# Scores of four steps in one block of 64x64 tiles, in a kernel of windowed attention and a two-layer MLP

## The chip, the core and the metric

The kernel runs on one core of one Trainium2 chip. A core has a matrix engine (TensorE, "PE" in the profile, with its weight loads as "PEld"), VectorE ("DVE"), ScalarE ("ACT"), GpSimd ("POOL") and SyncE ("SP"), each with its own queue of instructions, done in order. Matmuls read SBUF and write PSUM, which has eight banks of 128 partitions x 512 fp32 values. TensorE's 128x128 array can be split into tiles that work at the same time: a matmul on half of the columns writes 64 partitions, one on half of the rows reads 64 partitions. The metric is the device time of one execution in microseconds.

## What is computed

Attention with a symmetric window of 32 positions (8 batches, 8 heads, 576 tokens, 64 values a head), and on its output an MLP with a squared relu:

```python
scores = scale * np.matmul(q, k.transpose(0, 1, 3, 2))      # q, k, v: (8, 8, 576, 64)
mask = np.abs(pos[:, None] - pos[None, :]) <= 32
scores = np.where(mask, scores, -1000000000.0)
...
attn = np.exp(scores)
attn = attn / (np.sum(attn, axis=-1, keepdims=True) + 1e-09)
return np.matmul(attn, v).astype(np.float32)
...
x = np.ascontiguousarray(attn_out.transpose(0, 2, 1, 3)).reshape(B * S, H * D)   # (4608, 512)
r = np.maximum(x @ w_in, 0.0)                               # w_in: (512, 2048)
return (r * r @ w_out).astype(np.float32)                   # w_out: (2048, 512)
```

## The kernel before

**Attention steps.** The work of attention is cut into 72 steps, nine per batch: step n = 9 b + c takes 64 queries of all eight heads against 128 keys (64 queries plus 32 to each side; for even c the key halves are swapped). `scores` issues eight matmuls (L491), for four pairs of heads j and two key halves u, each with 64 weight columns of K on half of the array's columns and 128 moving columns of Q. K's 128 rows hold two heads, so Q (`QZ`) is kept twice for each pair, with zeros in the rows of the other head: columns 0 to 63 give the first head and 64 to 127 the second. The 128x512 result lies in one of two banks (`SC`). ScalarE takes its exp (L496) into `E`, VectorE multiplies by the mask (L503) into `PT`; both have two buffers. `av` does P V in eight matmuls of 65 columns, the last of which is the row sum (L518), into the bank `AVP`; VectorE takes the reciprocals (L530) and normalises (L532) into `XR`. `xturn` turns that so that the MLP can read it (`XT`, 32 slots of 64 tokens): on TensorE through the bank `TRP` and ScalarE for steps below 27 (L552, L557), and from 27 on, for two steps at once, by a transposing DMA on SP's queue (L543).

**Inputs.** For the first two batches K, Q and V come in pieces of 128 tokens (64 for the last), W1 in four chunks of 512 columns and W2 in four of 512 rows, all by DMAs that GpSimd issues in the order of the list `FIRST` ("k", "q", "v" with batch and piece, "e" the edge of V, "a" a W1 chunk, "b" a W2 chunk). K and Q of these batches are turned on TensorE through the score banks (`fine_turn`, L374). From the third batch on, GpSimd loads them raw, VectorE turns them in blocks of 32x32 (L451), and 16 DMAs a batch on SP's queue (`spread`, L465) bring them to their rows, in `KT` and `QZ`, which have two buffers each.

**MLP.** The 4608 tokens are nine tiles of 512. `mm1` is the first layer: a unit fills one of two banks `HT` (they alternate with the unit's number k), ScalarE does the relu (L581) into one of four buffers `RT`, and the square goes to VectorE, or to ScalarE for every second unit in the range `SQ` (L586). Tile 0 is done in 16 smaller units, in the order of `UNITS`: (first token, tokens, first block of the hidden width). Those of 128 tokens use the undivided array, all other matmuls of the kernel two column tiles. `mm2` is the second layer, four segments for each 128 tokens into one of two banks `OUTP`; ScalarE copies the result out and issues its DMA.

**Order.** Nothing of the order is written out by hand. Each instruction group is recorded with the tiles that it reads and writes, a guessed duration and a key; a planner (`Prog.schedule`) then plays the engines and DMA queues forward in time, takes on each engine the ready group with the smallest key, and adds 95 ns where TensorE's tiling changes. The resulting order is what each engine gets, with semaphore waits for what the tiles demand. While TensorE would have nothing to do at the start, it gets matmuls on the zero tile `ZZ`. The keys come from the constants at the head of the file: `LEAD` (how many steps attention runs ahead of the MLP), `LB` (a shift per batch), `QB`, `WB`, `VB`, `TB`, `GB`, `TST` and `SK` (when raw Q and K, V, its copies, the turns and the spreads of a batch are due), `FK`, `FQ`, `VK0`, `VK1` (pieces of the first batches), `KM`, `MD`, `TM` (MLP).

Of the kernel before, what the change touches and what calls it, by code (L numbers as in the profile page):

```python
# [5 lines left out]
ALU = mybir.AluOpType  # L6
ACTF = mybir.ActivationFunctionType
# [13 lines left out]
LEAD = 11  # L21
# [6 lines left out]
LB = (5.75, 0.0, -0.25, -3.0, -0.75, 3.75, 2.25, 1.0)  # L28
TB = (22.5, -1.0, -5.0, -4.5, 15.5, 29.5)
GB = (86.0, 56.0, 67.0, 42.0, 58.0, 11.0)  # L30
TST, SK = 0.7, -27.0
QB = (70.0, 34.0, 26.0, -78.0, 102.0, 86.0)
WB = (3.0, 26.0, 54.0, 80.0, 89.0, 54.0)
VB = (30.5, -13.5, 14.0, -32.5, 0.5, 0.5)
SQ = (16, 144, 2)
VENG = ('DVE', 'DVE', 'DVE')
KENG = ('DVE', 'ACT')
FK, FQ = 29.75, 18.0
VK0, VK1 = 9.25, 8.0
KM, MD, TM = -55.0, 8.0, 3.0  # L40
# [5 lines left out]
FIRST = (  # L46
# [222 lines left out]
class Gen:  # L269
# [5 lines left out]
    def alloc(self):  # L275
        nc = self.nc
        sb, ps = nc.alloc_sbuf_tensor, nc.alloc_psum_tensor
        self.SC = [ps(f"sc{i}", [128, 512], F32) for i in range(2)]
        self.AVP = ps("avp", [128, 512], F32)
        self.TRP = ps("trp", [128, 1024], BF16)  # L280
# [14 lines left out]
        self.E = [sb(f"e{i}", [128, 512], BF16) for i in range(2)]  # L295
        self.PT = [sb(f"pt{i}", [128, 512], BF16) for i in range(2)]
# [67 lines left out]
    def fine_turn(self, b, t, x, key):  # L364

        t0, n = PIECES[x]
        tag, ps = ("sc", t == "q"), self.SC[t == "q"][:]
# [112 lines left out]

    def scores(self, n):
        b, c = divmod(n, NCH)
        i = b % 2
        sc = self.SC[n % 2]
        key = n - LEAD + LB[b]

        def f(e):
            for j in range(4):
                for u in range(2):
                    at = 64 * c + 64 * (u if c % 2 else 1 - u)  # L490
                    mm = e.matmul(sc[64 * u:64 * u + 64, 128 * j:128 * j + 128], self.KT[i][:, j, at:at + 64],  # L491
                                  self.QZ[i][:, j, :, 64 * c:64 * c + 64], start=True, stop=True)
            return mm

        self.p.rec("PE", f, reads=self.qk_tags(b, c), writes=[("sc", n % 2)], key=key, dur=230, mode="col")
        self.p.rec("ACT", lambda e: e.activation(self.E[n % 2][:], sc[:], ACTF.Exp, scale=0.125),  # L496
                   reads=[("sc", n % 2)], writes=[("e", n % 2)], key=key, dur=600)
        mi = 0 if c % 2 else (2 if c == 0 else 3 if c == NCH - 1 else 1)
        msk = self.MASK[mi]
        pt = self.PT[n % 2][:].rearrange("p (h q) -> p h q", h=8)  # L500
        ee = self.E[n % 2][:].rearrange("p (h q) -> p h q", h=8)
        mb = bass.AP(msk, 0, [[64, 128], [0, 8], [1, 64]])
        self.p.rec("DVE", lambda e: e.tensor_tensor(pt, ee, mb, ALU.mult),  # L503
                   reads=[("e", n % 2), ("mask", mi)], writes=[("pt", n % 2)], key=key, dur=430)

    def av(self, n):
        b, c = divmod(n, NCH)
# [229 lines left out]
```

## Time and profile before

| | |
|---|---|
| median of 3 runs | 312.55 us (311.18 to 313.21) |
| the profiled execution | 312.32 us, its span in the profile 310.5 us |
| granted TensorE clock | 1.0 |
| matmuls and weight loads | 4117 of each |
| DMA traffic | HBM read 36.70 MB, written 9.44 MB |

A row of the groups reads: line, engine and operation, tile written <- tiles read, shape, count | busy us in all, mean ns of one | idle time just before them, and what ended most of it. A row of the timeline: start us, length us, engine, line, operation, tiles, shape, count. Matmuls overlap, so the length of a row exceeds the distance to the next start. A row of the stretches: from:to, its length, then for each engine that has such instructions (here PE, PEld, DVE, ACT) the busy us and count, then granted clock, DMA share and GB/s. A row of DMA issues: tiles, queue, count, KB each, median us from issue to landing.

### The profile page before, as it was taken

The numbers are of one execution on the slowest core, as the hardware profiler recorded it, in microseconds if no ns is written. First come the engines' busy times: TensorE is split into PE (matmuls) and PEld (weight loads), VectorE is DVE, ScalarE is ACT, GpSimd is POOL, SyncE is SP. The second block draws the span as 40 slices with busy tenths as digits, with TensorE's granted clock in tenths as the row PEclk, the third lists the DMA queues.
The fourth block names the chain that finished last, engine by engine and source line by source line (L and its number), as shares of the span: only waits on it lengthen the run. The fifth ranks groups of instructions, "written<-read, shape, count | busy, mean of one in ns | idle before, by whom it ended". The sixth has DMA issues, their size and how long they took to land.

```text
span 310.5 us, 9706 instructions
## 1 busy us (share of the span) xinstructions
PE 301.4 (97%) x4117; PEld 222.4 (72%) x4117; DVE 184.4 (59%) x460; ACT 200.9 (65%) x374; POOL 89.1 (29%) x129
## 2 busy tenths in 40 slices
PE   6879999999999999999999999999999999999996
PEld 2548887868977777776577777777777776776665
DVE  7667467957888988868859645688463232111000
ACT  2557698776866883588377857888746862675211
POOL 8999958331153242431222121000000000000000
PEclk9999999999999999999999999999999999999999
DMA  9999999999989989998889496314232012000112
GB/s 69 146 174 197 175 199 186 228 190 223 179 116 198 169 84 152 260 190 101 138 153 186 94 141 54 73 48 109 68 103 70 3 51 87 34 36 36 68 73 98
DMA packets 99226, 38.51 MB, mean 124 GB/s; under 512 B 71920, under 2 KB 94192, under 8 KB 99184
## 3 DMA queue, kind: packets, MB, share of 16 engines
q0 software_dynamic: 73664, 18.36, 62.7%
q1 hardware_dynamic: 20480, 10.36, 15.8%
q10 hardware_dynamic: 5040, 9.18, 9.1%
q8 instruction: 32, 0.52, 0.7%
q14 instruction: 10, 0.08, 0.1%
HBM read 36.70 MB, written 9.44 MB: 149 GB/s over the span
## 4 chain that ended last, share of the span: by engine, by line
PE 82%; DMA 7%; DVE 5%; POOL 4%; SPq 1%; issue 1%; ACT 0%; POOLq 0%; DVEq 0%
PE outp L62 37%; PE ht L62 33%; PE sc L491 5%; PE avp L518 3%; PE ht L60 3%; DMA vd<-in_v_dram 3%; DMA qz<-qst 2%; DVE kst L451 2%; DVE qst L451 2%; DMA kt<-kst 2%; POOL qfr L361 1%; SPq L465 1%; POOL kfr L361 1%; POOL vd L409 1%; PE trp L552 1%; PE sc L374 1%
## 5 line engine op out<-in xcount | busy, mean ns | idle before, releaser
L62 PE MATMUL outp<-w,gt 128*64 128x512 bf16 (+1 forms) x1184 | 140.4, 373 | 0.0
L62 PE MATMUL ht<-xt,w 128*64 128x512 bf16 (+1 forms) x1280 | 132.3, 348 | 0.5 <-issue 0.4
L581 ACT ACTIVATE rt<-ht 128x512 bf16<-128x512 f32 x144 | 85.3, 595 | 40.6 <-PE ht L62 35.4
L62 PEld LDWEIGHTS ht<-xt,w 128*64 128x64 bf16 x1280 | 93.5, 136 | 22.5 <-issue 1.3
L62 PEld LDWEIGHTS outp<-w,gt 128*64 128x64 bf16 x1184 | 74.7, 110 | 32.7
L586 DVE TENSOR_TENSOR gt<-rt 128x512 bf16<-128x512 bf16 x80 | 33.7, 422 | 47.9 <-ACT rt L581 40.4
L496 ACT ACTIVATE e<-sc 128x512 bf16<-128x512 f32 x72 | 41.6, 595 | 14.4 <-PE sc L491 8.7
L409 POOL DMA_DIRECT2D vd<-in_v_dram x32 | 29.2, 922 | 56.4 <-PE avp L518 37.1
L604 ACT ACTIVATE oe<-outp 128x512 f32<-128x512 f32 x35 | 20.9, 596 | 33.3 <-PE outp L62 33.1
L586 ACT ACTIVATE gt<-rt 128x512 bf16<-128x512 bf16 x64 | 40.4, 631 | 1.5 <-PE outp L62 0.3
L451 DVE STREAM_TRANSPOSE kst<-kraw 128x256 bf16<-128x256 bf16 (+1 forms) x48 | 36.7, 828 | 1.8 <-DMA kt<-kst 1.8
L451 DVE STREAM_TRANSPOSE qst<-qraw 128x256 bf16<-128x256 bf16 (+1 forms) x48 | 35.6, 833 | 1.8 <-DMA qz<-qst 1.8
L530 DVE RECIPROCAL rs<-avp 128x4 f32<-128x4 f32 x72 | 13.0, 181 | 35.2 <-PE avp L518 34.6
L503 DVE TENSOR_TENSOR pt<-e,mask 128x512 bf16<-128x512 bf16 x72 | 29.6, 412 | 5.8 <-ACT e L496 4.8
L532 DVE TENSOR_TENSOR xr<-avp,rs 128x256 bf16<-128x256 f32 x72 | 30.3, 420 | 1.1
L491 PE MATMUL sc<-qz,kt 128*64 128x128 bf16 x576 | 26.5, 220 | 0.9 <-DVE kt L384 0.6
L491 PEld LDWEIGHTS sc<-qz,kt 128*64 128x64 bf16 x576 | 22.4, 110 | 6.4 <-DVE kt L384 1.1
L417 POOL DMA_DIRECT2D vx<-in_v_dram x16 | 10.1, 630 | 32.4 <-PE sc L491 17.0
L429 DVE COPY vx<-vd 64x528 bf16<-64x528 bf16 (+1 forms) x28 | 16.4, 586 | 3.9 <-DMA vd<-in_v_dram 3.4
L400 POOL DMA_DIRECT2D kraw<-in_k_dram x24 | 14.9, 689 | 10.4 <-DVE kst L451 10.4
L400 POOL DMA_DIRECT2D qraw<-in_q_dram x24 | 15.1, 703 | 4.1 <-DVE gt L586 2.8
L390 ACT ACTIVATE qz<-sc,half 128x512 bf16<-128x512 bf16 (+1 forms) x20 | 12.0, 644 | 6.5 <-PE sc L374 6.3
(43 smaller groups left out, 160.8 us busy)
## 6 DMA issues: line engine op xcount, KB each, us to landing
out_dram<-oe ACTq DMA_DIRECT2D x35, 256.0 KB, 2.8
vd<-in_v_dram POOLq DMA_DIRECT2D x32, 128.0 KB, 6.2
kraw<-in_k_dram POOLq DMA_DIRECT2D x24, 144.0 KB, 12.7
qraw<-in_q_dram POOLq DMA_DIRECT2D x24, 144.0 KB, 10.9
kt<-kst SPq DMA_DIRECT2D x48, 72.0 KB, 4.0
qz<-qst SPq DMA_DIRECT2D x48, 72.0 KB, 4.0
w<-in_moe_w_in_dram POOLq DMA_DIRECT2D x4, 512.0 KB, 10.2
w<-in_moe_w_out_dram POOLq DMA_DIRECT2D x4, 512.0 KB, 16.1
```

The lines of the kernel that those rows point to most:

```text
L62: mm = e.matmul(out[r:r + 64], w[:, r:r + 64], x, start=start, stop=stop)
L400: self.p.rec("POOL", lambda e, g=g, s=s: e.dma_start(raw[32 * g:32 * g + 32], s), writes=[("raw", t, b % 2, g)], dma=(f"{t}{b % 2}", b), k ...
L409: self.p.rec("POOL", lambda e, s=s: e.dma_start(self.VD[i][:, s, :, 0:64], v[b, :, 32 + 128 * s:160 + 128 * s, :].rearrange("h p d -> p h ...
L429: self.p.rec(on, lambda e, d=dst, c=src: e.tensor_copy(d, c) if on == "DVE" else e.activation(d, c, ACTF.Copy), reads=rd, writes=[("vxc", ...
L451: self.p.rec("DVE", lambda e: e.transpose(dst, src), reads=[("raw", t, i, g) for g in range(4)], writes=[("st", t, dh, m0)], key=key, dur= ...
L491: mm = e.matmul(sc[64 * u:64 * u + 64, 128 * j:128 * j + 128], self.KT[i][:, j, at:at + 64], self.QZ[i][:, j, :, 64 * c:64 * c + 64], star ...
L496: self.p.rec("ACT", lambda e: e.activation(self.E[n % 2][:], sc[:], ACTF.Exp, scale=0.125), reads=[("sc", n % 2)], writes=[("e", n % 2)], ...
L503: self.p.rec("DVE", lambda e: e.tensor_tensor(pt, ee, mb, ALU.mult), reads=[("e", n % 2), ("mask", mi)], writes=[("pt", n % 2)], key=key, ...
L532: self.p.rec("DVE", lambda e: e.tensor_tensor(bass.AP(xr, o, [[512, 128], [64, 4], [1, 64]]), bass.AP(self.AVP, 0, [[512, 128], [VE, 4], [ ...
L581: self.p.rec("ACT", lambda e: e.activation(rt[:], ht[:], ACTF.Relu), reads=[("ht", k % 2)], writes=[("rt", k % 4)], key=key, dur=600)
L586: self.p.rec(on, lambda e: e.tensor_tensor(dst, rr, rr, ALU.mult) if on == "DVE" else e.activation(dst, rr, ACTF.Square), reads=[("rt", k ...
L604: self.p.rec("ACT", lambda e: e.activation(oe[:], op[:], ACTF.Copy), reads=[("outp", x % 2)], writes=[("oe", x % 3)], old=[("mtmp", 0), (" ...
```

## The change

The scores of steps 32 to 71 are made in groups of four steps. A group is one block of 64 matmuls on four tiles of 64x64: the array's row halves r hold the two heads of a pair, so that each head's 64 rows of K meet only its own 64 rows of Q, and the zeros in `QZ` aren't read. A matmul has 64 moving columns in place of 128. The row halves write to different banks of a pair. There are two pairs: the two score banks, and a second one from the banks of the row turns and of P V; the group's first two steps go to the first pair and the other two to the second. The exp of a step then reads 256 values from each bank of its pair, and what follows finds its columns in another order. `E` and `PT` get four buffers each. Steps below 32 are computed as before.

```diff
+    def score_group(self, n0):
+        def f(e):
+            for n in range(n0, n0 + 4):
+                b, c = divmod(n, NCH)
+                kt, qz, sc = self.KT[b % 2], self.QZ[b % 2], self.PAIR[n // 2 % 2]
+                o = 256 * (n % 2)
+                for j in range(4):
+                    for u in range(2):
+                        at = 64 * c + 64 * (u if c % 2 else 1 - u)
+                        for r in range(2):
+                            mm = e.matmul(sc[64 * u:64 * u + 64, r, o + 64 * j:o + 64 * j + 64], kt[64 * r:64 * r + 64, j, at:at + 64],
+                                          qz[64 * r:64 * r + 64, j, r, 64 * c:64 * c + 64], start=True, stop=True)
+            return mm
...
+        self.p.rec("PE", f, reads=list(dict.fromkeys(rd)), writes=[("sc", 0), ("sc", 1), "trp", "avp"],
+                   key=n0 - LEAD + LB[n0 // NCH] - GK, dur=448, mode="quad")
...
+        else:
+            if n % 4 == 0:
+                self.score_group(n)
+            sc, tags = self.PAIR[n // 2 % 2][:, :, 256 * (n % 2):256 * (n % 2) + 256], [[("sc", 0), ("sc", 1)], ["trp", "avp"]][n // 2 % 2]
...
-                self.scores(n)
-                self.av(n)
-                self.xturn(n)
+                if n < NG:
+                    ns = [n]
+                elif n % 4 == 3:
+                    ns = range(n - 3, n + 1)
...
+                for n in ns:
+                    self.scores(n)
+                for n in ns:
+                    self.av(n)
+                    self.xturn(n)
```

A relu that overwrites a buffer which ScalarE itself has squared now waits for that square by semaphore:

```diff
+        if k % 4 in self.squared:
+            relu.deps.add(self.squared.pop(k % 4))
```

And the constants of the planner are others; the order of every engine comes out anew. Those that the text speaks of:

```diff
-LEAD = 11
+LEAD = 12
...
-TST, SK = 0.7, -27.0
+TST, SK = 0.8, 5.0
...
-SQ = (16, 144, 2)
+SQ = (12, 112, 2)
...
+NG, GK = 32, -5.0
...
 UNITS = (
-    (0, 128, 0), (128, 128, 4), (128, 128, 12), (128, 128, 8), (256, 256, 2), (0, 128, 4), (256, 256, 6),
-    (256, 256, 10), (256, 256, 12), (256, 256, 14), (0, 128, 8), (256, 256, 0), (128, 128, 0), (0, 128, 12),
-    (256, 256, 4), (256, 256, 8),
+    (128, 128, 12), (0, 128, 0), (256, 256, 0), (128, 128, 4), (256, 256, 12), (256, 256, 4), (256, 256, 10),
+    (0, 128, 12), (128, 128, 8), (256, 256, 14), (0, 128, 4), (128, 128, 0), (256, 256, 2), (0, 128, 8),
+    (256, 256, 6), (256, 256, 8),
 )
 FIRST = (
-    ("v", 0, 1), ("k", 0, 0), ("q", 0, 0), ("k", 0, 2), ("q", 0, 1), ("k", 0, 1), ("v", 0, 2), ("q", 0, 2),
-    ("q", 0, 3), ("v", 0, 0), ("q", 1, 1), ("e", 0, False), ("a", 0, 2), ("k", 1, 2), ("v", 0, 3),
-    ("k", 0, 3), ("a", 0, 1), ("q", 0, 4), ("v", 1, 3), ("k", 0, 4), ("a", 0, 0), ("a", 0, 3), ("k", 1, 0),
-    ("b", 0, 0), ("q", 1, 0), ("k", 1, 1), ("e", 0, True), ("q", 1, 2), ("k", 1, 4), ("v", 1, 0),
-    ("e", 1, False), ("k", 1, 3), ("b", 0, 1), ("b", 0, 2), ("v", 1, 2), ("v", 1, 1), ("e", 1, True),
-    ("b", 0, 3), ("q", 1, 3), ("q", 1, 4),
+    ("q", 0, 0), ("k", 0, 0), ("q", 0, 1), ("k", 0, 2), ("q", 0, 2), ("k", 0, 1), ("k", 0, 3), ("v", 0, 0),
+    ("q", 0, 3), ("v", 0, 1), ("k", 1, 1), ("v", 0, 2), ("e", 0, False), ("a", 0, 3), ("v", 0, 3),
+    ("q", 0, 4), ("k", 0, 4), ("a", 0, 0), ("q", 1, 0), ("q", 1, 1), ("a", 0, 1), ("v", 1, 3), ("k", 1, 0),
+    ("e", 0, True), ("v", 1, 0), ("k", 1, 2), ("a", 0, 2), ("b", 0, 2), ("e", 1, False), ("b", 0, 1),
+    ("e", 1, True), ("q", 1, 3), ("v", 1, 2), ("v", 1, 1), ("b", 0, 0), ("q", 1, 2), ("k", 1, 3), ("q", 1, 4),
+    ("k", 1, 4), ("b", 0, 3),
 )
```

More of the change, by code (lines that the diff above doesn't have):

```diff
@@ L294, in alloc @@
         self.ID = sb("ident", [128, 128], BF16)
[L295 to L296 removed]
+        self.E = [sb(f"e{i}", [128, 512], BF16) for i in range(4)]
+        self.PT = [sb(f"pt{i}", [128, 512], BF16) for i in range(4)]
         self.RS = [sb(f"rs{i}", [128, 4], F32) for i in range(2)]
@@ L483, in scores @@
         i = b % 2
-        sc = self.SC[n % 2]
         key = n - LEAD + LB[b]
[L487 to L495, printed above, removed]
@@ L496, in scores, with f @@
-        self.p.rec("ACT", lambda e: e.activation(self.E[n % 2][:], sc[:], ACTF.Exp, scale=0.125),
-                   reads=[("sc", n % 2)], writes=[("e", n % 2)], key=key, dur=600)
+        ex = self.E[n % 4][:]
+        if n < NG:
+            sc, tags = self.SC[n % 2], [("sc", n % 2)]
+            def f(e):
+                for j in range(4):
+                    for u in range(2):
+                        at = 64 * c + 64 * (u if c % 2 else 1 - u)
+                        mm = e.matmul(sc[64 * u:64 * u + 64, 128 * j:128 * j + 128], self.KT[i][:, j, at:at + 64],
+                                      self.QZ[i][:, j, :, 64 * c:64 * c + 64], start=True, stop=True)
+                return mm
+            self.p.rec("PE", f, reads=self.qk_tags(b, c), writes=tags, key=key, dur=230, mode="col")
+        else:
+            if n % 4 == 0:
+                self.score_group(n)
+            sc, tags = self.PAIR[n // 2 % 2][:, :, 256 * (n % 2):256 * (n % 2) + 256], [[("sc", 0), ("sc", 1)], ["trp", "avp"]][n // 2 % 2]
+            ex = ex.rearrange("p (r x) -> p r x", r=2)
@@ L498, in scores @@
+        self.p.rec("ACT", lambda e: e.activation(ex, sc, ACTF.Exp, scale=0.125),
+                   reads=tags, writes=[("e", n % 4)], key=key, dur=600)
         mi = 0 if c % 2 else (2 if c == 0 else 3 if c == NCH - 1 else 1)
         msk = self.MASK[mi]
-        pt = self.PT[n % 2][:].rearrange("p (h q) -> p h q", h=8)
-        ee = self.E[n % 2][:].rearrange("p (h q) -> p h q", h=8)
+        pt = self.PT[n % 4][:].rearrange("p (h q) -> p h q", h=8)
+        ee = self.E[n % 4][:].rearrange("p (h q) -> p h q", h=8)
@@ L580, in mm1 @@
         us = range(t0 // 128, (t0 + n) // 128)
-        self.p.rec("ACT", lambda e: e.activation(rt[:], ht[:], ACTF.Relu), reads=[("ht", k % 2)],
-                   writes=[("rt", k % 4)], key=key, dur=600)
+        relu = self.p.rec("ACT", lambda e: e.activation(rt[:], ht[:], ACTF.Relu), reads=[("ht", k % 2)],
+                          writes=[("rt", k % 4)], key=key, dur=600)
+        if k % 4 in self.squared:
+            relu.deps.add(self.squared.pop(k % 4))
         rr = rt[:].rearrange("p (d t) -> p d t", d=nd)
```

55 lines of the change are left out of this document (31 added, 24 removed).

## The prediction

> **What bounds the kernel now.** I read the page's busy table and chain of waits first, to see which engine sets the end, and then the groups by shape, to see how much of that engine's time the scores hold.
>
> ```profile
> span 310.5 us, 9706 instructions
> PE 301.4 (97%) x4117; PEld 222.4 (72%) x4117; DVE 184.4 (59%) x460; ACT 200.9 (65%) x374; POOL 89.1 (29%) x129
> ...
> PE 82%; DMA 7%; DVE 5%; POOL 4%; SPq 1%; issue 1%; ACT 0%; POOLq 0%; DVEq 0%
> ...
> L62 PE MATMUL outp<-w,gt 128*64 128x512 bf16 x1120 | 136.9, 379 | 0.0
> L62 PE MATMUL ht<-xt,w 128*64 128x512 bf16 x896 | 108.4, 380 | 0.5 <-issue 0.4
> L491 PE MATMUL sc<-qz,kt 128*64 128x128 bf16 x576 | 26.5, 220 | 0.9 <-DVE kt L384 0.6
> ```
>
> TensorE is the bound: 97% busy, 82% of the chain. Its rows hold almost no idle time (0.5 and 0.9 us). "Busy" counts overlapping matmuls, though, so what a block really costs is read from start to start in the timeline, in a stretch without a wait:
>
> ```profile
> 177.79 0.42 PE L491 MATMUL sc<-qz,kt 128*64 128x128 bf16 x8
> 178.01 0.32 PE L518 MATMUL avp<-vx,pt 128*64 128x65 bf16 x8
> 178.14 1.06 PE L62 MATMUL outp<-w,gt 128*64 128x512 bf16 x8
> 179.00 0.42 PE L491 MATMUL sc<-qz,kt 128*64 128x128 bf16 x8
> ```
>
> One step's scores cost 0.22 us, one step's P V 0.13, eight matmuls of 512 columns 0.86. So 2016 of the long matmuls take 2016 x 0.86/8 = 217 us and 72 score blocks 72 x 0.22 = 16 us. Time that TensorE is spared in the packed part comes off the span one for one. The next view says where the packed part begins: the idle-filling matmuls on the zero tile, by stretch.
>
> ```profile
> 0.00:20.00 20.00, 12.49 (x75) 4.64 (x77) 0.27 (x1) 0.91 (x4) 1.00 1.62 120
> 20.00:40.00 20.00, 4.44 (x32) 1.45 (x28) 0.00 (x0) 0.00 (x0) 1.00 1.69 188
> 40.00:310.00 270.00, 0.00 (x0) 0.00 (x0) 0.00 (x0) 0.00 (x0) 1.00 0.77 120
> ```
>
> Fillers stand only before 40 us, 4.44 us of them between 20 and 40. There the kernel has spare TensorE time; after it, next to none.
>
> **The tiles, part one: the block itself.** Steps 32 to 71 are 40 steps, ten groups. A group drops 4 x 8 matmuls of 128 columns, 4 x 0.22 = 0.89 us, and adds 64 of 64 columns on four tiles, 16 rounds of four. No 64-row tile is in this trace. The nearest row is a block with 64 moving and 64 weight columns on two tiles:
>
> ```profile
> 53.62 0.29 PE L374 MATMUL sc<-ident,kfr 128*64 128x64 bf16 x8
> 53.74 0.39 PE L62 MATMUL outp<-w,gt 128*64 128x512 bf16 x2
> ```
>
> Eight in 0.12 us, 0.0305 us a round of two, weights hidden. If four tiles run as two do, a group is 16 x 0.0305 = 0.49 us. Bounds: at half of a score block it is 4 x 0.11 = 0.45; if the two row halves don't overlap, it is 32 rounds, 0.98; and if the sequencer's rate in the P V block above (16 weight loads and matmuls in 0.13 us, 8 ns each) is its best, 128 instructions take 1.02. I take 0.49, as that row has the same shape. The page "TensorE: Matmul & The Clock Gate" of the Trainium skill, Part 3, puts packed tiles about 4 ns apart; by an estimate from it, 128 instructions would take 0.51 us and the change would keep its gain. The trace's 8 ns stretch has only two tiles to fill, so it is no proof of a limit, but no row here shows 4 ns either.
>
> **Part two: the mode switches.** The group stands between two-tile blocks, so it costs two changes of tiling. Where the first MLP tile changes between 128x128 and two tiles, the trace shows such changes:
>
> ```profile
> 40.84 0.41 PE L491 MATMUL sc<-qz,kt 128*64 128x128 bf16 x8
> 41.19 1.08 PE L60 MATMUL ht<-xt,w 128*128 128x128 bf16 x16
> 42.20 0.41 PE L491 MATMUL sc<-qz,kt 128*64 128x128 bf16 x8
> 42.45 0.39 PE L62 MATMUL ht<-xt,w 128*64 128x256 bf16 x4
> ```
>
> The score block ahead of the change takes 0.35 us in place of 0.22: 0.12 to 0.13 for a change. Two per group are 0.24. The bounds are nothing (if that gap is special to 128x128) and 0.3. The page "TensorEngine Tiling (Array Packing)" of the Trainium skill, Key Properties, says that a changed tiling mode drains the engine; it speaks against the change, and would charge these 20 changes as the row does.
>
> So a group costs 0.49 + 0.24 = 0.73 against 0.89: 0.16 to 0.17 saved, **1.7 us over ten groups**, with +3.7 us (1.02 + 0.24 = 1.26) as the bad end and -2.4 (0.45 + 0.2) as the good one.
>
> **What hangs on the group.** The exp of a step reads two banks in place of one, still 128x512; P V reads the same number of columns in another order: nothing. The group writes both the score pair and the pair that holds P V's output, so P V of its first step now waits for the exps of its third and fourth. Queued behind that on ScalarE are relus, and behind P V's wait on TensorE the MLP matmuls, which the written order puts ahead where it can.
>
> ```profile
> L496 ACT ACTIVATE e<-sc 128x512 bf16<-128x512 f32 x72 | 41.6, 595 | 14.4 <-PE sc L491 8.7 <-DVE pt L503 5.6
> L586 ACT ACTIVATE gt<-rt 128x512 bf16<-128x512 bf16 x64 | 40.4, 631 | 1.5 <-PE outp L62 0.3
> L586 DVE TENSOR_TENSOR gt<-rt 128x512 bf16<-128x512 bf16 x80 | 33.7, 422 | 47.9 <-ACT rt L581 40.4 <-PE outp L62 7.1
> ```
>
> Four exps are 2.4 us; TensorE needs about 3.9 us a step (the packed 280 us, from 30 us on, over 72 steps), so 15 us a group: the MLP covers the wait. If the cover fails, as where MLP work runs out before a tile's input is there, each such place costs up to those 2.4 us. Squares on ScalarE go from 64 to 50 (units 12 to 111, every second): 14 x 0.631 = 8.8 us less there and 14 x 0.422 = 5.9 us more on VectorE; both are far from full, so nothing. The relu's new wait names a square four units (some 3.5 us of MLP work) back, long done: nothing, else one relu's delay. The spread DMAs on SP move earlier (SK), past the turns of x on the same queue; the group that joins two batches asks for the second one's K and Q one to three steps sooner. I cost both at nothing with 1 us either way, for the waits after 40 us are few already; the longest:
>
> ```profile
> 152.69 1.89 PE L62 MATMUL outp<-w,gt 128*64 128x512 bf16 x16
> 155.02 1.30 PE L62 MATMUL ht<-xt,w 128*64 128x512 bf16 x10 [0.44 <-issue]
> ```
>
> **The new order at the start.** This is the other term. First-tile units alternate between two PSUM banks, so unit k can't pass unit k-2. Loads land in order of issue; here are the four W1 chunks (2, 1, 0, 3 in that order): issue times, then time to landing in the same order.
>
> ```profile
> 11.61 0.85 POOL L436 DMA_DIRECT2D w<-in_moe_w_in_dram  x1
> 14.97 0.88 POOL L436 DMA_DIRECT2D w<-in_moe_w_in_dram  x1
> 17.97 1.65 POOL L436 DMA_DIRECT2D w<-in_moe_w_in_dram  x2
> ...
> w<-in_moe_w_in_dram POOLq DMA_DIRECT2D x1, 512.0 KB, 7.9
> w<-in_moe_w_in_dram POOLq DMA_DIRECT2D x1, 512.0 KB, 9.6
> w<-in_moe_w_in_dram POOLq DMA_DIRECT2D x1, 512.0 KB, 10.9
> w<-in_moe_w_in_dram POOLq DMA_DIRECT2D x1, 512.0 KB, 12.6
> ...
> 25.71 1.08 PE L60 MATMUL ht<-xt,w 128*128 128x128 bf16 x16
> 27.58 1.07 PE L60 MATMUL ht<-xt,w 128*128 128x128 bf16 x16
> ...
> 29.34 1.98 PE L60 MATMUL ht<-xt,w 128*128 128x128 bf16 x32
> 31.25 0.32 PE L518 MATMUL avp<-vd,pt 128*64 128x65 bf16 x8
> ```
>
> The chunks land at 19.5, 24.6, 28.9 and 31.3 us (the last was issued near 18.7). Unit 0 needs chunk 0 and unit 1 chunk 1, so the chunk that lands first lies idle, and the first unit runs at 25.71, after chunk 1. A chunk alone takes 31.3 - 28.9, about 2.5 us; between the first two lie a chunk and three pieces of 128 rows, so a piece takes (5.1 - 2.5)/3 = 0.87. With these rates the new list lands chunk 3 at 20.4 (one piece more ahead of it), chunk 0 at 24.7, chunk 1 at 28.9, chunk 2 at 35.2. Its unit 0 needs chunk 3, units 1 and 2 chunk 0, unit 4 chunk 3 again. Units cost 1.91/2 = 0.95 us: by 32.6 us, where the old one has done four, the new one could have done seven or eight: 3.5 units, 3.3 us ahead at most. Against that, chunk 2 comes 3.9 us later than the last one did, and units of both banks need it: of the 16, nine can run before, done near 33.6, and until 35.2 about 1.6 us find only scores and turns. Net 3.3 - 1.6 = **1.7 us** gained, with ends at 3.4 (the second batch's work fills the hole) and 0 (steps 2 and 3, which unit 0 needs, come no sooner, or the W2 chunk that the second layer opens with, now behind 11 more loads, makes TensorE wait).
>
> **Sum.** The profiled execution took 312.3 us (span 310.5 and 1.8 around it; the median of the runs is 312.55): 312.3 - 1.7 - 1.7 = 308.9.
>
> **The rivals.** First, *the tiles pay, the start doesn't*: other waits on loads take over before 40 us. For it: the DMA queue there is full, and V's and W2's chunks still close it. Against it: 4.44 us of fillers. 312.3 - 1.7 = 310.6.
>
> Second, *the four tiles don't run as four*: either the row halves take turns, so that the change doesn't do what it says, or the sequencer can't feed them at 3.8 ns an instruction. The place is each of the ten blocks, the price +0.37 each, +3.7 us, from a block longer than 0.65 us on it costs more than it saves. For it: the 8 ns stretch, and no row with four tiles. Against it: in the 64-column block, starts on two tiles do overlap with weights hidden. 312.3 + 3.7 = 316.0 with a flat start.
>
> Third, *input for the MLP comes late*: P V in fours delays the turn of x, on which the MLP tile waited at 155.02 already. Five tiles after the switch, each up to 2.4 us late, half of it covered: +6, less 3.4, 314.9. Against it: 15 us a group.
>
> **How the numbers follow.** Main case 0.60, first rival 0.19, second 0.12, third 0.09. The main case's own range is 306 to 310.5, from the good ends and from a head of 0.1. A measurement of this kernel tells about 1% (3.1 us) from no change, so faster means under 309.4: five sixths of the main case, 0.50; within 1%: the rest of it and the first rival, 0.29; slower: 0.21. The likeliest is 308.9; the range that leaves out 2 in 10 runs from 305.8 to 316.0.
>
> **What would show it.** Ten score blocks of 64 matmuls after 32 steps, 0.49 us from start to start and a 0.12 gap on either side (right), or near 1.0 (second rival). The first 128x128 unit near 21 to 22 us, and fillers between 20 and 40 us of 2 to 3 us (right), or still above 4 (first rival). Waits of the first-layer matmuls of a microsecond or more after 130 us: third rival. The forecast is wrong if the block exceeds 0.65 us or TensorE is not packed after 40 us.

## The result, and the profile after

| | before | after |
|---|---|---|
| median | 312.48 us (310.79 to 313.70, 18 executions) | 314.25 us (312.32 to 317.55, 18 executions) |
| ratio to before | 1 | 1.0055, 95% interval 1.0032 to 1.0078 |
| profiled execution, its span | 312.32, 310.5 us | 313.82, 311.9 us |

The change makes the kernel a little slower, by half a per cent. The scores did become cheaper; the time comes back as waits of the MLP. Below, ratios are always to the kernel before on the same chip. Times are medians of all executions, while ratios leave out those more than 1.5% above the fastest of their kernel (one of the 18 of after, three of the 12 of e15).

The page of after, its busy table and its chain of waits:

```profile
PE 301.9 (97%) x4441; PEld 196.4 (63%) x4441; DVE 192.9 (62%) x474; ACT 193.3 (62%) x360; POOL 89.4 (29%) x129
...
PE 86%; POOL 6%; DMA 5%; issue 1%; DVE 1%; ACT 0%; POOLq 0%
```

TensorE is as busy as it was, and bounds the kernel as before. The groups by shape say more:

```profile
L63 PE MATMUL ht<-xt,w 128*64 128x512 bf16 x896 | 107.9, 381 | 3.2 <-issue 2.4 <-DMA xt<-xr 0.8
...
L492 PE MATMUL ta<-qz,kt 64*64 64x64 bf16 x320 | 4.6, 193 | 0.0
...
L492 PE MATMUL sc<-qz,kt 64*64 64x64 bf16 x320 | 4.5, 195 | 0.0
```

The last two rows are the new blocks, 640 matmuls, ten times 64. The first is where the time is lost: in front of the first layer of the MLP (L63, `ht`), TensorE stood idle for 3.2 us, where the row before the change says 0.5. The difference, 2.7 us, is more than the blocks save.

**The blocks.** One group in the timeline of TensorE, the one of steps 44 to 47:

```profile
166.71 1.49 PE L63 MATMUL ht<-xt,w 128*64 128x512 bf16 x12
168.13 0.45 PE L492 MATMUL sc<-qz,kt 64*64 64x64 bf16 x32
168.40 0.44 PE L492 MATMUL ta<-qz,kt 64*64 64x64 bf16 x32
168.77 1.52 PE L63 MATMUL ht<-xt,w 128*64 128x512 bf16 x12
```

Twelve matmuls of 512 columns need 12 x 0.1075 = 1.29 us (0.86 for eight), but the block starts 1.42 us after the first of them, so the way into it costs 0.13. From its start to the next work are 0.64 us. Together 0.77 for what cost 0.89: 0.12 us saved. Eight of the ten blocks are like this one; two (at 120.0 and 256.9 us) take 0.75 and 0.79 in place of 0.64, for a reason that the rows don't show, so the ten save some 0.9 us. Half of the block takes 0.27 us from start to start, so a round of four matmuls takes some 0.03 us: the four tiles do run at the same time.

**The start.** The same view from 24 to 36 us, with the fillers on the zero tile (`zz`) and the first units of the MLP:

```profile
24.37 1.98 PE L61 MATMUL ht<-xt,w 128*128 128x128 bf16 x32
...
26.53 0.28 PE L579 MATMUL ta<-ident,xr 128*64 128x128 bf16 x4
...
26.77 1.25 PE L63 MATMUL outp<-zz 128*64 128x512 bf16 x10
...
28.01 0.60 PE L63 MATMUL outp<-zz 128*64 128x512 bf16 x4
28.46 0.30 PE L579 MATMUL ta<-ident,xr 128*64 128x128 bf16 x4
28.70 1.08 PE L61 MATMUL ht<-xt,w 128*128 128x128 bf16 x16
29.71 0.30 PE L579 MATMUL ta<-ident,xr 128*64 128x128 bf16 x4
29.85 0.60 PE L63 MATMUL outp<-zz 128*64 128x512 bf16 x4
...
30.88 0.30 PE L579 MATMUL ta<-ident,xr 128*64 128x128 bf16 x4
...
32.42 1.94 PE L63 MATMUL ht<-xt,w 128*64 128x256 bf16 x32
```

The first two units start at 24.37, not at 21 to 22. After the third, at 28.70, TensorE has only fillers and the small blocks of single steps until 32.42. The rows of four matmuls at L579 are the turns of x, one step each: what lacks here is x of steps 4 to 7, which the first units of 256 tokens read. P V of step 7 ran at 27.85 already, but the turns share one bank, out of which ScalarE copies each, and follow each other every 1.2 us or so (28.46, 29.71, 30.88). The fillers' own time, in the view by stretch (PE, PEld, DVE and ACT behind the length):

```profile
20.00:40.00 20.00, 5.62 (x36) 1.75 (x36) 0.00 (x0) 0.00 (x0) 1.00 1.65 188
```

5.62 us between 20 and 40, where it was 4.44: more spare time of TensorE, not less.

**The waits.** The first-layer matmuls behind an idle time, in the timeline of TensorE from 100 us on:

```profile
124.38 1.03 PE L63 MATMUL outp<-w,gt 128*64 128x512 bf16 x8
126.17 1.95 PE L63 MATMUL ht<-xt,w 128*64 128x512 bf16 x16 [0.76 <-DMA xt<-xr]
...
156.40 0.29 PE L545 MATMUL ta<-vx,pt 128*64 128x65 bf16 x8
158.05 1.95 PE L63 MATMUL ht<-xt,w 128*64 128x512 bf16 x16 [1.35 <-issue]
...
184.75 2.78 PE L63 MATMUL outp<-w,gt 128*64 128x512 bf16 x24
188.62 1.08 PE L63 MATMUL ht<-xt,w 128*64 128x512 bf16 x8 [1.08 <-issue]
```

These are the starts of the MLP tiles 3, 4 and 5, each with the row ahead of it. From start to start, less the work between, they lose 0.93, 1.52 and 1.28 us, 3.7 in all. In the kernel before the same three places lose 0.19, 0.61 (the prediction shows these rows) and 0.22 us, 1.0 in all. Its rows for tiles 3 and 5:

```profile
124.18 1.92 PE L62 MATMUL outp<-w,gt 128*64 128x512 bf16 x16
126.09 1.95 PE L62 MATMUL ht<-xt,w 128*64 128x512 bf16 x16
...
184.25 0.32 PE L518 MATMUL avp<-vd,pt 128*64 128x65 bf16 x8
184.60 1.95 PE L62 MATMUL ht<-xt,w 128*64 128x512 bf16 x16
```

After 190 us TensorE waits for nothing in either kernel. Tile 3 starts at 126.1 us in both, when x of step 31 lands, so all that stands ahead of it has brought nothing: a lead of under half a microsecond of work at 60 us ends there. From there to its end after takes 185.76 us, 1.34 more than before. The waits at tiles 4 and 5 are 2.0 us longer in after, and the nine blocks behind 126 us save some 0.9; that makes 1.1, and 0.2 us stay unaccounted for. Tile 3 itself reads steps 24 to 31, none of which is in a group.

What ends such a wait can be followed back for tile 5. The timeline of all engines in after:

```profile
171.77 0.59 ACT L522 ACTIVATE e<-ta 128x512 bf16<-128x512 f32 x1
...
174.36 0.59 ACT L522 ACTIVATE e<-ta 128x512 bf16<-128x512 f32 x1
...
175.73 0.30 PE L545 MATMUL ta<-vx,pt 128*64 128x65 bf16 x8
...
180.15 5.35 SPq L570 DMA_TRANSPOSE xt<-xr  x2
...
182.15 0.30 PE L545 MATMUL ta<-vx,pt 128*64 128x65 bf16 x8
```

The group was scored at 168.1. The exps of its last two steps (`e<-ta`), which free the pair that P V writes, stand between relus and squares and end at 172.4 and 175.0. P V of step 44 comes at 175.73, of step 47 at 182.15. The second of the two turns is issued at 183.2 and, by the view of DMA issues, lands 5.4 us later:

```profile
xt<-xr SPq DMA_TRANSPOSE x1, 5.4
```

at 188.6, when tile 5 starts. The planner counts 3.4 us from issue to landing of a turn (`HWCALM`), and 2.4 us more when by its plan GpSimd's queue has a load under way (`HWLOAD`). With the constants of after it has 3.4 us for each of the turns of steps 31, 39 and 47, where the trace has 5.2, 6.6 and 5.4; with those of before it has 5.1, 3.9 and 4.8, where the trace has 6.3, 5.1 and 5.3. It puts the tile within a microsecond of the landing that it counts.

### The profile page after: what moved, and what is told of

It is laid out like the page before. It is cut to its first block, busy times and chain, and to the rows that moved or that the text cites. A ratio compares the mean times of both kernels' runs of the same rounds, so it can differ in the third digit from the quotient of the medians.

```text
span 311.9 us, 10349 instructions
## 1 busy us (share of the span) xinstructions
PE 301.9 (97%) x4441; PEld 196.4 (63%) x4441; DVE 192.9 (62%) x474; ACT 193.3 (62%) x360; POOL 89.4 (29%) x129
## 4 chain that ended last, share of the span: by engine, by line
PE 86%; POOL 6%; DMA 5%; issue 1%; DVE 1%; ACT 0%; POOLq 0%
PE outp L63 38%; PE ht L63 38%; DMA vd<-in_v_dram 4%; PE ta L545 3%; POOL qfr L362 2%; PE sc L512 2%; DMA xt<-xr 2%; POOL kfr L362 2%; PE ht L61 2%; PE sc L492 1%; POOL vd L410 1%; PE ta L492 1%; PE ta L579 1%; POOL w L437 1%; PE sc L375 1%
## 5 line engine op out<-in xcount | busy, mean ns | idle before, releaser
L63 PE MATMUL outp<-w,gt 128*64 128x512 bf16 (+1 forms) x1184 | 137.6, 374 | 0.0
L63 PE MATMUL ht<-xt,w 128*64 128x512 bf16 (+1 forms) x1280 | 131.8, 349 | 3.2 <-issue 2.4
L63 PEld LDWEIGHTS ht<-xt,w 128*64 128x64 bf16 x1280 | 82.9, 137 | 33.6 <-issue 3.0
L63 PEld LDWEIGHTS outp<-w,gt 128*64 128x64 bf16 x1184 | 64.8, 110 | 46.3 <-issue 0.7
L615 DVE TENSOR_TENSOR gt<-rt 128x512 bf16<-128x512 bf16 x94 | 39.4, 419 | 40.9 <-ACT rt L608 40.2
L522 ACT ACTIVATE e<-sc 128x512 bf16<-128x512 f32 x52 | 29.1, 597 | 12.7 <-PE ta L492 7.4
L557 DVE RECIPROCAL rs<-ta 128x4 f32<-128x4 f32 x72 | 13.1, 183 | 32.6 <-PE ta L545 32.0
L615 ACT ACTIVATE gt<-rt 128x512 bf16<-128x512 bf16 x50 | 31.6, 632 | 1.0
L559 DVE TENSOR_TENSOR xr<-ta,rs 128x256 bf16<-128x256 f32 x72 | 30.5, 424 | 1.5
L545 PEld LDWEIGHTS ta<-vx,pt 128*64 128x64 bf16 x320 | 11.1, 111 | 7.0 <-DVE xr L559 1.1
L63 PE MATMUL outp<-zz 128*64 128x512 bf16 x100 | 15.1, 388 | 0.0
```

The costliest lines, as they stand in the source:

```text
L63: mm = e.matmul(out[r:r + 64], w[:, r:r + 64], x, start=start, stop=stop)
L522: self.p.rec("ACT", lambda e: e.activation(ex, sc, ACTF.Exp, scale=0.125), reads=tags, writes=[("e", n % 4)], key=key, dur=600)
L545: mm = e.matmul(self.PAIR[1][64 * u:64 * u + 64, 1, VE * j:VE * j + VE], pt[:, p0 + 64 * u * w:p0 + 64 * u * w + 64], vt[:, h, 0:VE], star ...
L559: self.p.rec("DVE", lambda e: e.tensor_tensor(bass.AP(xr, o, [[512, 128], [64, 4], [1, 64]]), bass.AP(self.PAIR[1], 512, [[1024, 128], [VE ...
L615: op = self.p.rec(on, lambda e: e.tensor_tensor(dst, rr, rr, ALU.mult) if on == "DVE" else e.activation(dst, rr, ACTF.Square), reads=[("rt ...
```

## The experiments

Theory A: the tiles pay, and the late input of the MLP takes it back and more. Rivals: the four-tile block itself or what it does to PSUM loses the time (B); the loads on the DMA queues do, not the order.

**The tiles.** e1 leaves the order of the kernel after as it is and makes the blocks as before, 128 moving columns with the zeros, on two tiles.

```diff
-                        for r in range(2):
-                            mm = e.matmul(sc[64 * u:64 * u + 64, r, o + 64 * j:o + 64 * j + 64], kt[64 * r:64 * r + 64, j, at:at + 64],
-                                          qz[64 * r:64 * r + 64, j, r, 64 * c:64 * c + 64], start=True, stop=True)
+                        mm = e.matmul(sc[64 * u:64 * u + 64, n % 2, 128 * j:128 * j + 128], kt[:, j, at:at + 64],
+                                      qz[:, j, :, 64 * c:64 * c + 64], start=True, stop=True)
```

> The changed kernel with every instruction in the same place, but each block of four steps is made of 32 matmuls of 128 columns on two tiles, zeros included, as before the change. Theory A (the four-tile block pays a little, the input of the MLP comes too late): a block costs 4 x 0.22 = 0.89 us in place of some 0.77 with its two tiling changes, so about 1 us slower than the changed kernel, near 315.3, with the same waits for x near 125, 157 and 187 us. Theory B (the four-tile blocks or their tiling changes are what costs): faster than the changed kernel by 1 us or more, near 313 or less. Theory C (the constants and the order alone): no word on the block; the same waits, as in A.

314.34 us, ratio 1.0078 (1.0049 to 1.0108). That is 0.2% above after, which the intervals don't separate, but not the microsecond below it that B asks for; B is false. In its trace TensorE waits at the same three places, with idle times of 0.56, 0.76 and 1.38 us, so the four tiles don't make the waits.

**The waits.** e2 takes the wait for x away: MLP tiles 3, 4 and 5 read the tokens of the tile before (so these outputs are other tokens'), with the order of after. e3 does it to the kernel before, e5 to e1.

```diff
+EARLY = (3, 4, 5)
...
-        x0 = s0 % RX
+        x0 = (s0 - 8 if T in EARLY else s0) % RX
```

> The changed kernel in the same planned order, but MLP tiles 3, 4 and 5 read the tokens of the tile before them, which are long there, so that their first matmuls don't wait for x (their outputs are other values). Theory A: the waits of 0.96, 1.52 and 1.28 us at 125, 157 and 187 us go, 3.8 us in all, and the time falls by 3 to 3.8 us to 310.5 to 311.3, unless another wait takes their place. Theory B (the blocks): at most 1 us is gained, as TensorE would soon wait for something else or the loss lies in the blocks, 313.3 or more.

> The kernel before with the same edit: MLP tiles 3, 4 and 5 read the tokens of the tile before them. Theory A: it loses only its own waits for x, 0.19, 0.63 and perhaps 0.2 us, so 0.8 to 1 us, near 311.6, and the changed kernel without its waits is then the faster of the two by 0.5 to 1.3 us. Theory B: it stays faster than the changed kernel with the same edit.

> The changed kernel in its own planned order, with both edits: blocks of four steps on two tiles, and MLP tiles 3, 4 and 5 reading the tokens of the tile before them (their outputs are other values). With no wait for x to swallow it, the worth of the four tiles shows in the time. Theory A: a block costs 0.89 us in place of 0.77, so 1.2 us over 310.36 (the four-tile kernel with the same edit), 311.3 to 311.8. If the four tiles are worth nothing: 310.4.

e2: 310.36 us, 0.9952 (0.9934 to 0.9971); e3: 311.62, 0.9988 (0.9965 to 1.0011); e5: 312.58, 0.9996 (0.9977 to 1.0016). The groups by shape of e2 have the row

```profile
L64 PE MATMUL ht<-xt,w 128*64 128x512 bf16 x896 | 107.7, 381 | 0.0
```

So the waits cost after 1.0055 - 0.9952 = 1.0%, 3.2 us, and before 0.1%. Without them the change gains 0.36%, 1.1 us (the intervals of e2 and e3 overlap a little). And four tiles against two, with nothing to swallow it, are worth 0.9996 - 0.9952 = 0.44%, 1.4 us by the ratios, give or take 0.8, where the timeline says 0.9.

**Groups or order?** e4 begins the groups at step 48, behind the three waits; e6 has none. Both have the constants of after (`NG` = 48, 72) and are planned anew.

> The changed kernel with groups only from step 48 on, after the last tile that waited for its input (the rest is planned anew with the same constants). Theory A, in its narrow form (the groups of steps 32 to 47 delay P V and so x): the waits near 157 and 187 us shrink to below 0.8 us each, and with six groups still saving some 0.1 us each the time is 312 to 312.8. Theory C (the constants are to blame, with groups or without): waits of 3 us and more stay, 314 or more.

> The changed kernel's constants with no groups at all: every step's scores alone on two tiles, the rest planned anew. Narrow A (the groups make x late): the waits for x at the starts of MLP tiles 3, 4 and 5 fall to some 1 us in all and the time is 312 to 313. Theory C (the constants make it late, groups or not): waits of 3 us or more, 314.5 or more.

e4: 317.19 us, 1.0153 (1.0112 to 1.0194); e6: 316.37, 1.0099 (1.0064 to 1.0134). Theory C came out in both. e4 is slower than after; the intervals of e6 and after overlap. The wait at 187 us is gone in both, but the two before it stay, and the first has grown: 2.4 us at 125 in e4 and 2.9 us at 125.7 in e6, where x of step 31 takes 8.8 and 9.3 us to land. The second loses 0.7 us in e4 and 1.4 at 155.5 in e6, which has not one group in it. (e4 has one more, 1.43 us at 216, in front of a group that waits until VectorE has emptied P V's bank.) So the constants of after make x late by themselves; groups are not the only cause. They were chosen for an order with groups, though, so e6 doesn't tell what single steps cost at their best. In e4 the wait brought something that was not in any expectation. Its stretches, to be read as before with GpSimd as a fifth engine (the last three numbers are granted clock, DMA share, GB/s), and the matmuls of that place in its timeline:

```profile
125.00:127.80 2.80, 0.57 (x14) 0.34 (x11) 2.49 (x6) 0.20 (x1) 0.88 (x1) 0.99 2.81 125
127.80:131.20 3.40, 3.40 (x18) 1.65 (x20) 0.45 (x1) 1.23 (x2) 2.42 (x4) 0.51 1.26 265
```

```profile
127.78 3.57 PE L63 MATMUL ht<-xt,w 128*64 128x512 bf16 x16 [2.23 <-issue]
131.17 1.04 PE L63 MATMUL outp<-w,gt 128*64 128x512 bf16 x8
```

After 2.2 us of idleness the granted clock is 0.51 for 3.4 us, and sixteen matmuls take 3.4 us from start to start in place of 1.7. The wait costs its own 2.2 us and 1.7 on top.

**The load on the queues.** e10 and e11 leave out the 24 raw loads of K and Q of batches 5 to 7 (these batches then use earlier ones) in after and before, order unchanged.

```diff
+        gone = {o for o in p.ops if o.dma is not None and o.dma[0] in ("k0", "k1", "q0", "q1") and o.dma[1] in LEFT}
+        p.ops = [o for o in p.ops if o not in gone]
```

> The changed kernel in its own planned order with the 24 raw loads of K and Q of batches 5, 6 and 7 left out (those batches are computed from the K and Q of earlier ones). If what holds x up is the DMA engines, busy with these loads while x is turned: the turns of x for steps 31, 39 and 47 land 2.5 to 3.5 us after their issue in place of 5.2, 6.6 and 5.4, the three waits fall from 3.8 us to 1.5 or less, and the time is 311 to 312. If it is P V coming late behind the groups: the waits stay above 3 us, near 314.

> The kernel before with the same 24 loads left out. If the DMA engines hold x up: its own waits of 0.2, 0.6 and 0.2 us go, 311 to 311.8, and the changed kernel with the same edit is as fast or up to 1 us faster. If P V behind the groups is the cause, the changed kernel stays the slower one by 1 us or more.

e10: 313.22 us, 1.0022 (1.0002 to 1.0043); e11: 311.58, 0.9976 (0.9955 to 0.9997). The loads cost both kernels about the same (0.33% and 0.24%), and after stays behind by 0.46%: these 24 loads are not the difference between the two. They do hold x up. In e11 the three turns land in 3.6, 4.1 and 3.9 us, and none of the three waits is left. In e10 neither expectation came true as a whole: the turn of step 31 lands in 2.5 us and the wait at tile 3 is gone, but the turns of steps 39 and 47 still take 6.2 and 6.1 us, with 0.81 and 1.82 us of idle time behind them (in a traced execution that was the slowest of its twelve, 315.04 us). While these two were under way a load of V and several writes of results were too, which e10 leaves in. So load on the DMA engines is not ruled out as what makes a landing long; no run took the loads of V away.

**The coupling of P V to the later exps.** e14 exchanges the pairs: a group's first two steps go to the pair that P V shares. P V of the first step then waits for the exps of two steps only.

```diff
-                kt, qz, sc = self.KT[b % 2], self.QZ[b % 2], self.PAIR[n // 2 % 2]
+                kt, qz, sc = self.KT[b % 2], self.QZ[b % 2], self.PAIR[1 - n // 2 % 2]
```

> The kernel after with the two pairs of banks exchanged in the groups: the first two steps of a group write their scores to the pair that P V also uses, the last two to the score pair, so P V of the first step waits for the exps of the first two steps only. The planner orders the work again with the same constants; by its plan only some steps move, P V of steps 44 to 47 about 4 to 5 us forward (44: 171.6 to 166.5, 47: 178.1 to 173.8), while 39 and 31 stay. Theory A (the input of the MLP tile is late because P V waits for exps through the shared pair): the DMA for steps 46 and 47 is issued some 4 us earlier, the wait at 187 us falls from 1.3 us to under 0.3 us, that at 157 us stays near 1.5 us and that at 125 us near 1 us, and the time falls by about 1 us: 313.0 us, ratio 1.000 to 1.003. Theory B (the DMA is late because of load on its queue, wherever it is issued): the wait at 187 us stays above 1 us, the time stays at 314.2 us, ratio 1.0055. Against both: the earlier P V brings the wait forward to a place in the groups, with the time unchanged.

313.86 us, 1.0044 (1.0011 to 1.0077). Locally theory A is right. The timeline of all engines in e14, to be compared with that of after:

```profile
170.85 0.29 PE L545 MATMUL ta<-vx,pt 128*64 128x65 bf16 x8
...
174.63 0.59 ACT L522 ACTIVATE e<-sc 128x512 bf16<-128x512 f32 x1
...
178.22 0.30 PE L545 MATMUL ta<-vx,pt 128*64 128x65 bf16 x8
...
179.92 1.28 SPq L570 DMA_TRANSPOSE xt<-xr  x1
```

P V of step 44 runs at 170.85, ahead of the last exp, and that of step 47 at 178.22, 3.9 us earlier than in after; the turn is issued at 179.92 and lands 2.8 us later. The wait at 187 us is gone. But the whole is hardly faster, as the last of the three cases expected, though its new wait is not in a group. The waits of the first layer in the timeline of TensorE:

```profile
126.64 1.95 PE L63 MATMUL ht<-xt,w 128*64 128x512 bf16 x16 [0.81 <-DMA xt<-xr]
157.46 1.95 PE L63 MATMUL ht<-xt,w 128*64 128x512 bf16 x16 [1.15 <-issue]
245.45 1.08 PE L63 MATMUL ht<-xt,w 128*64 128x512 bf16 x8 [1.00 <-issue]
```

A new wait stands at 245: the order there, planned anew, puts a tile again at the moment at which the planner counts x as landed, 3.9 us after its issue, and x of step 63 took 5.4 us. The coupling makes one wait, not the loss.

**Constants searched with slower landings.** e7 is the kernel after, e9 the kernel before, each with constants searched so that the order still holds when DMAs land 1 to 3 us later than the planner counts. e12 puts groups from step 48 into e9's constants; e13 is e9 again, beside it on the same chip. e15 and e16 put groups with exchanged pairs into it, from steps 40 and 48. In e12, e15 and e16 the constants of the later batches are searched again.

> The changed kernel's code, groups and tiles with other constants, chosen so that the planned order still holds when DMAs land 1 to 3 us later than the planner counts on and a block with its two tiling changes costs 0.76 us. If late x is what the change lost by, and groups as such can live with it: no wait over 1 us at the starts of MLP tiles 3 to 5, and 309.5 to 311, below the kernel before. If groups make x late in any order: 313 or more.

> The code before the change, no groups, with constants chosen in the same way as for the replanned groups. If the order alone makes the difference: 310 to 311, as fast as the replanned groups. If the four tiles are worth their 0.12 us a group: 1 to 1.5 us slower than the replanned groups, 310.5 to 312.

> Groups and four tiles only for steps 48 to 71, on the replanned constants of the kernel without groups, which are kept for the first five batches; those of the last three are chosen anew. If four tiles pay where x is not due at once: no wait over 0.8 us behind 190 us, six groups save 0.12 to 0.15 us each, so 0.7 to 0.9 us below the kernel without groups that runs beside it. If groups make x late in any order: a wait of 1 us or more at the start of MLP tile 6, 7 or 8, and no gain.

> The replanned kernel without groups once more, beside the one with groups from step 48 on. It was 0.9951 of the kernel before; 0.993 to 0.997 again, in either theory.

> The best version with single steps (e9 and e13, ratio 0.995) with groups of four steps from step 40 on, the pairs of banks exchanged as in e14, and the constants of the later batches searched again with slower landings of x. Theory A (groups are worth 0.14 us each wherever the input of the MLP isn't late, and the exchanged pairs keep it from being late): eight groups take off 1.1 us, no wait for x beyond those of e9 (0.4 to 0.6 us each at two places), ratio 0.990 to 0.993. Theory B (in groups the work before a tile comes in lumps, so what they save comes back as waits, at whatever place the order is tight): waits of 1 us or more appear that e9 hasn't, ratio 0.995 or above.

> As e15, with groups from step 48 on (six groups). After step 47 no wait for x was seen behind 190 us in the kernel after nor in e12, so the groups lie where TensorE has the most other work. Theory A: six groups take off 0.8 us, ratio 0.992 to 0.993. Theory B: ratio 0.995 to 0.998 as in e12 (0.9976), with waits near 138 and 151 us that come from the new order of the batches around them.

| | us | ratio (95% interval) |
|---|---|---|
| e7, groups from 32 | 314.09 | 1.0025 (0.9992 to 1.0058) |
| e9, single steps | 310.92 | 0.9951 (0.9926 to 0.9976) |
| e13, single steps | 310.96 | 0.9948 (0.9926 to 0.9971) |
| e12, groups from 48 | 311.62 | 0.9976 (0.9949 to 1.0003) |
| e15, groups from 40 | 313.25 | 0.9985 (0.9952 to 1.0018) |
| e16, groups from 48 | 312.24 | 0.9971 (0.9944 to 0.9998) |

The constants alone (the order, and which engine does a square), without a single four-tile block, make the kernel 0.5% faster than before, twice over: e9 is the best version found, and beats both kernels. Its profiled execution loses 0.4 us at the start of tile 4 and 0.6 at tile 5. e7 missed what was expected of it; in its trace TensorE still waits 2.15 us ahead of a unit at 56.0 us and 1.09 ahead of tile 5 at 186.5. No version with groups beats e9, e12 neither, of which a gain was expected; the intervals of e12, e15 and e16 overlap with that of e9. In e15 and e16 theory B came true; TensorE in the timeline of e15, then of e16:

```profile
189.25 3.01 PE L71 MATMUL ht<-xt,w 128*64 128x512 bf16 x16 [2.10 <-DMA xt<-xr]
```

```profile
153.13 3.44 PE L71 MATMUL ht<-xt,w 128*64 128x512 bf16 x16 [2.12 <-DMA xt<-xr]
```

In e15 x of step 47 was issued at 183.5 (e9: 179.6) and landed 5.6 us later; in e16 x of step 39 was issued at 146.0, ahead of e9's 149.6, but took 7.0 us. By plan the two were to land 3.4 and 3.6 us after their issue. Each wait is over 2 us, and behind each the granted clock is 0.50 for 3.4 us, so that the sixteen matmuls take 3.01 and 3.44 us in place of 1.95.

## Why the prediction was wrong

It said 308.9 us, and the kernel takes 314.25: on the other side of before. That this lies in the range is in part luck, as the range's upper end, 316.0, is the price of the second rival, which the blocks rule out.

**The bound, and the block: right, with the size nearly half off.** The tiles run four at a time; the block with its two switches costs 0.77 us where the sum had 0.73, and saves 0.12 in place of 0.17; two blocks of the ten save nothing. Over ten groups 0.9 us came by the timeline in place of 1.7. The second rival, with tiles that take turns, is false. The 8 ns per instruction that spoke for it was no limit of the sequencer: 64 weight loads and 64 matmuls take 2 x 0.27 = 0.54 us, 4.2 ns each. In the trace the four matmuls of a round start 3 to 4 ns apart. The rule of the Trainium skill that the prediction weighed there ("TensorE: Matmul & The Clock Gate", Part 3: packed tiles about 4 ns apart) agrees with that. The next round starts 32 ns later all the same, much like the 30.5 ns of a round of two, which has half as many instructions. This suggests that the block's time follows the 64 columns rather than the count of instructions. The Trainium skill ("TensorEngine Tiling (Array Packing)", Key Properties) says that a change of tiling drains the engine; the 0.13 us ahead of each block agrees.

**The start: wrong.** The step that failed is "could have done seven or eight" units by 32.6 us, which asked only when W1's chunks land. These came as worked out, at 19.6, 24.3, 28.6 and 34.7 us by issue and landing, against 20.4, 24.7, 28.9 and 35.2. But unit 0 needs x of step 3, not turned until 23.3, and four of the first eight units have 256 tokens and need x of steps 4 to 7, whose turns wait one behind the other until 30.88. By 32.4 us after has done three units, where before has done four. Of the 1.7 us forecast there was at most 0.5 us at 60 us and nothing left behind 126 us. The text named "steps 2 and 3 ... come no sooner" as its bad end; it did not ask about steps 4 to 7, which by the rows decided; no run tested it. The first rival had this outcome, and its sign, fillers above 4 us, is there with 5.62; but it blamed loads, and what lacks is x.

**The waits: wrong, and this made the sign.** The step that failed is "the MLP covers the wait", with mid-run waits costed at nothing. The 15 us a group of MLP work is there, but it is not what stands in front of a tile's start. There the fixed order of TensorE has the tile's first matmuls next, and the chain exp, P V, normalise, turn, landing is on the path. The waits at tiles 3, 4 and 5 lose 3.7 us where 1.0 was lost before, and without them after is 1.0% faster (e2). Nor do four exps take "2.4 us": in the group of steps 44 to 47 they stand among relus and squares and last from 169.05 to 174.95, 5.9 us. The third rival had late input as its mechanism; its chance of 0.09 was too low. That its time, 314.9, is the nearest is in part luck: it added 6 us of waits and took off 3.4 of gains, where the timeline shows 2.7 and about 0.9, and it looked at five tiles behind the switch, of which two waited, while tile 3, ahead of it, waited too. Its reason was half right: P V waits for later exps (e14 shows it at one tile), but the searched constants make x late even with single steps (e6).

The smaller terms held: 50 squares are left on ScalarE and 94 on VectorE, as counted, and no wait for a square or for K and Q of a group's second batch shows in the rows of after.

The row that could have told was in the prediction: the wait at 155.02 us. By the DMA issues of that trace x of step 39 lands at 154.9, so the kernel before already starts tile 4 at the moment at which x lands. At such a place an order that is shorter by plan gains nothing, and 1 us of lateness costs 1 us.

What is shown: four tiles are worth some 0.4% where no wait swallows it (e2, e5); the waits for x cost after about 1% (e2) and make the sign. They don't come of the tiles (e1), and x is late with these constants even without groups (e6); the coupling of P V makes one of the waits (e14), and one went with the 24 loads (e10). What stays open: how much of the long landings is the load of the other transfers, and whether an order with groups exists in which x is never late; four searches (e7, e12, e15, e16) found none that beats single steps.

## What to carry to other kernels

Before crediting a saving on the busiest engine, look for the places at which that engine already starts the moment an input lands: up to the next such place the saving is only worth what the input's chain becomes shorter. A planner that counts a transfer at less than it takes under load (here 3.4 us for 5 to 7) puts the consumer exactly into that gap; an order searched against the longer landing was worth 0.5% with the old matmuls, though how much of it is due to the landing and how much to more searching was not separated. And when work is batched in fours, follow the last of the four to whoever waits for it.

## What the runs showed of the hardware

- A wait of TensorE of 2.1 to 2.8 us in the middle of the packed part was followed by a granted clock of 0.50 for 3.41 us in four traces (e4, e6, e15, e16); waits up to 1.8 us never were, and one of 2.15 us (e7, at 56 us) was not. The traces show why. In e6 the clock falls twice, and the stretches at full clock between its changes, 17.07, 102.4 and 184.3 us, are 5, 30 and 54 times 3.41 us; the other traces show such multiples too. So time runs in windows of 3.41 us, and what counts is how long TensorE idles within one. Three windows of e6, then two of e7 (TensorE's busy time comes first, the granted clock third from the end):

```profile
124.66:128.07 3.41, 1.25 (x20) 0.64 (x14) 2.21 (x5) 0.60 (x1) 0.88 (x1) 1.00 2.90 89
128.07:131.49 3.42, 2.82 (x14) 1.27 (x16) 1.43 (x3) 0.82 (x2) 2.25 (x4) 0.50 1.28 268
131.49:134.90 3.41, 3.41 (x40) 2.10 (x38) 1.28 (x4) 2.14 (x5) 0.15 (x1) 1.00 1.62 221
```

```profile
51.20:54.62 3.42, 2.69 (x59) 2.14 (x56) 1.87 (x6) 2.84 (x6) 2.73 (x5) 1.00 1.47 194
54.62:58.03 3.41, 1.99 (x52) 1.99 (x53) 0.97 (x3) 1.14 (x3) 0.38 (x1) 1.00 2.13 164
```

In e6 a window with 2.16 us of idle time is followed by one at half clock. In e7 the wait lies across the border, 0.73 us on one side and 1.42 on the other, and the clock stays. Of the windows of the 14 traces that hold the clock, all with 1.81 us of idle time or more (seven, ahead of the kernel's last microseconds) were followed by one at half clock, and none with 1.76 or less was. So a wait of 2.2 us can cost nearly twice its length, as in e4, or only its length. Four of the 17 executions of after behind its ratio have a mean granted clock of 0.995; they took 314.2 to 316.0 us, some 1.7 us more than the others, which is what one such window would cost. Where in the kernel it fell isn't known, as none of the four was traced. The Trainium skill ("TensorE: Matmul & The Clock Gate", Part 1 and Why this matters for your kernels) tells of half the clock after an idle window of about 3.4 us, of windows that run freely, and warns of gaps above about 3 us. The half clock, its 3.4 us and the free run of the windows agree with these traces; the length of the gap does not, 1.8 us within a window were enough.
- A round of four 64x64 tiles with 64 columns takes 31.5 to 32 ns with its four weight loads, much as a round of two does (30.5). Going into the block costs 0.13 us, and coming out of it about 0.1.
- The landing of a transposing DMA ranges from 2.4 to 8.3 us after its issue in after, for transfers of the same size, and up to 10.6 us in e6.
